# The first 512 tokens' q and k multiplied in f32 from the landed rows, six of nine blocks, held in PSUM until the scale is known

## The chip, the cores and the metric

The kernel runs on one core of one Trainium2 chip. The metric is device time in microseconds (us), the time of one launch of the whole program. Two kernels are compared by runs on the same chip, and one execution of each is recorded by the hardware profiler. Five engines work in parallel, each through its own instructions in order: TensorE (PE in the profile, with its weight loads as PEld) multiplies matrices into the eight banks of PSUM, VectorE (DVE), ScalarE (ACT) and GpSimd (POOL) work on elements, and SyncE (SP) issues most of the DMAs.

## The reference

Two independent operators over 2048 tokens of 576 features each, whose outputs stand side by side:

```
a: qkv = x @ wqkv                    x (2048, 576), wqkv (576, 1728)
   32 heads of 18; scores = q k^T / sqrt(18), only where 0 <= i - j < 256
   a = softmax(scores) v @ wo
b: K[d, l] = Re sum_n C[d,n] exp(dt_d A[d,n] l) dt_d B[d,n]     n = 0..127, l = 0..2047
   b = causal convolution over l of u (2048, 576) with K, plus u * Dskip
```

All inputs and outputs are f32.

## The kernel before

**Stages.** The program has a front (inputs, scales, splits of operands), a stage in which the projection qkv of operator a (`proj`), the tables and taps of K of operator b (`tables`) and the first step of the transform of u (`s1_u`) run together, and then the attention, into which the rest of the convolution and the output projection are woven.

**The projection.** A product of f32 operands is made from three products of f16 operands. An operand is multiplied by a power of two that depends on its largest absolute value, rounded to f16 (`wh`, `xh`), and the rest is kept in a second f16 tile (`wl`, `xl`). `mm14` (L173) makes one block: 128 columns of wqkv against 512 tokens, over 576 rows in five slices (the fifth has 64 rows, stored twice, so that its second half can carry a residual): five products wh xh, five wl xh and four wh xl, 14 in all, into one bank. A chunk of 512 tokens has nine blocks of q and k (m = 0 to 8) and four of v (tk = 0 to 3, two halves of 288 columns each, operands exchanged). A q/k block leaves its bank as f16 plus residual, one ScalarE and one VectorE instruction (L345, L346), and goes to DRAM by six DMAs of SP (`store_heads`). There are four chunks.

**The scales** need the largest value of all of wqkv and of all of x. `front` (L217) loads wqkv in four parts of 432 columns (the K tile, L229), the first 512 tokens of x transposed (`raw`, four tiles, L240) and the other 1536 tokens flat (`flat`, four pieces in two buffers, L237). VectorE reduces each as it lands (`amax`), GpSimd reduces over the partitions (`pow2_max`), VectorE makes the power of two (`pow2_of`). `split_w` makes wh on ScalarE and wl on VectorE, `split_x` the same of x. Between them stand the `level` steps, which split the exponents of operator b into three bf16 parts by way of small DMAs on the queues of ScalarE and GpSimd (into `al` and `ps`), and the first exponentials (`exps_ab`, `exps_q`): an outer product on PE (L376) into one of two xps banks, then an Exp on ScalarE (L393).

**What sets the order.** The front is under `manual_schedule`: its instructions keep the order in which they are written, on each engine and queue. Of the next stage only the order of the generators' steps is written (`merge`, first six steps of `proj` and four of `tables`, then 50, 308 and 16 of `proj`, `tables`, `s1_u`); the planner orders the instructions by its own costs and may start some while the front still runs. Each engine then takes its instructions in that fixed order. The attention is under `manual_schedule` again.

**PSUM.** Eight banks in the shared stage: pps 3 (projection and s1_u), xps 2 (outer products), trig 2 (sn and cs, which ScalarE writes for the tables), kps 1 (kp, the taps).

**The tables.** For each of 36 groups c: `factors` (two outer products, a fraction on ScalarE and VectorE, two Sin, then GpSimd, L424 to L435), `phases`, `qtable` (Sin into sn and cs, four VectorE products into Q), `products` (two GpSimd instructions, L446) and `taps` (64 small f32 products on PE into kp, L484). After every second group kp goes to the tile K (L490), which lies in the room that held wqkv.

The lines that matter beside the functions below are these, of `front`:

```python
for c in range(4):
    nc.sync.dma_start(wf[:, c], a["wqkv"][:, c])
...
    if c == 1:
        raw = [self.load_x(e, "prep", "raw%d" % e) for e in range(4)]
...
for e in range(4):
    self.split_x(raw[e], self.xs, e)
self.split_w(2, 0)
self.split_w(3, 0)
```

## Time and profile before

| what | value |
|---|---|
| median of 3 runs | 989.41 us (987.56 to 995.23) |
| the profiled execution | 989.74 us, span 988.0 us |
| busy in the span | PE 834.1, VectorE 666.0, GpSimd 567.5, ScalarE 565.7 us |
| mean granted clock of PE | 0.977 |
| scale of the weights known | 31.09 us |
| scale of x known | 49.98 us |
| first q/k block on PE | 53.06 us |
| last taps leave kp | 411.4 us |

The span runs from the first instruction to the last; the execution's own time has a little more around it. In a row of instructions stand the start in us, the time in us, engine, line, operation, output<-inputs, shapes and count, and in brackets the idle time before it and what ended it. Rows of groups (line first) have the busy us and the mean ns of one, then the idle time before. PE's products are pipelined and their ends are modelled, so products overlap in the rows and the distance of their starts says more than their length. The row of a transposing or splitting helper has the helper's line, not its caller's.

### The profile page before, as it was taken

Reading aid. Unit: us, or ns where it says so; the run is one execution under the profiler, and the core shown is the slowest. Engines: PE = TensorE matmul, PEld = TensorE weight load, DVE = VectorE, ACT = ScalarE, POOL = GpSimd, SP = SyncE. Lnnn points to the kernel's source line nnn. Section 1 sums busy time; section 2 is a strip of 40 time slices with the busy share of each in tenths; the row PEclk is TensorE's granted clock in tenths of the full one; section 3 lists DMA queues with packets and bytes.
Section 4 is the critical chain, followed back from the end, with each engine's and each line's share of the span. In section 5 each row is a group of like instructions: output and inputs, shape, how many; then the busy total and the mean of one; then the engine's idle time right before and its main releaser. Section 6 shows DMA issues by size and latency. Waiting matters only on the chain.

```text
span 988.0 us, 26891 instructions
## 1 busy us (share of the span) xinstructions
PE 834.1 (84%) x10364; PEld 443.4 (45%) x10364; DVE 666.0 (67%) x1784; ACT 565.7 (57%) x917; POOL 567.5 (57%) x674
## 2 busy tenths in 40 slices
PE   0287979898899899889988888888888899999987
PEld 0033645465457466644433333333333344444445
DVE  5689496556754774666586788788777766667534
ACT  1455756557767666325655655665556555665770
POOL 2118575465875785802257775866686756644460
PEclk9999989899999999999999999999999999999999
DMA  9825535344444343354584675756755664387663
GB/s 307 255 57 138 124 93 146 87 98 116 102 104 120 89 106 107 106 185 151 170 156 120 165 190 137 172 144 167 179 137 143 158 194 104 108 223 196 205 195 130
DMA packets 137177, 145.34 MB, mean 147 GB/s; under 512 B 36552, under 2 KB 105336, under 8 KB 136280
## 3 DMA queue, kind: packets, MB, share of 16 engines
q1 hardware_dynamic: 131000, 131.45, 49.6%
q0 software_dynamic: 4592, 10.32, 3.8%
q10 hardware_dynamic: 1456, 1.84, 0.6%
q8 instruction: 82, 1.34, 0.6%
q14 instruction: 47, 0.39, 0.1%
HBM read 81.29 MB, written 61.01 MB: 144 GB/s over the span
## 4 chain that ended last, share of the span: by engine, by line
PE 47%; DVE 20%; issue 11%; ACT 7%; DMA 7%; POOL 6%; SPq 2%; DVEq 0%; ACTq 0%; POOLq 0%
PE pp L180 9%; PE po L764 6%; PE r L700 5%; PE r L974 5%; PE kp L484 4%; PE pp L525 3%; PE r L566 3%; PE r L574 3%; PE ST L741 3%; DVE jk L707 3%; PE x L376 2%; PE r L525 2%; POOL P L752 2%; ACT P L743 2%; DMA c_ct<-in_c_ct_dram 2%
## 5 line engine op out<-in xcount | busy, mean ns | idle before, releaser
L707 DVE CUSTOM_DVE_ANT_0 jk<-r,bias 128x288 f32<-128x288 f32 (+7 forms) x512 | 199.8, 433 | 92.8 <-PE r L700 88.3
L752 POOL TENSOR_SCALAR_AFFINE_SELECT P<-P 128x512 f32<-128x512 f32 x240 | 166.3, 722 | 156.6 <-ACT P L743 154.2
L743 ACT ACTIVATE P<-ST,esc 128x1024 f32<-128x1024 f32 (+1 forms) x192 | 202.0, 1059 | 84.2 <-PE ST L741 83.9
L446 POOL TENSOR_TENSOR m<-A,tr 128x1024 f32<-128x1024 f32 x72 | 144.2, 2025 | 83.6 <-PE kp L484 77.7
L700 PE MATMUL r<-K,qb 128*64 128x288 f16 (+7 forms) x1024 | 130.0, 294 | 36.8 <-DVE qb L691 12.2
L700 PEld LDWEIGHTS <-qb 128*64 128x64 f16 x1024 | 57.6, 108 | 122.2 <-issue 68.5
L764 PE MATMUL po<-P,V 128*32 128x256 f32 (+2 forms) x1408 | 100.0, 396 | 13.3 <-ACT osb L772 5.1
L603 POOL TENSOR_TENSOR Y<-t,t 64x288 f32<-64x288 f32 x64 | 55.1, 861 | 66.0 <-DVE t L598 64.0
L484 PE MATMUL kp<-Q,m 128*32 128x64 f32 x4608 | 80.6, 222 | 10.2 <-ACT K L490 2.6
L484 PEld LDWEIGHTS kp<-Q,m 128*32 128x32 f32 x4608 | 69.4, 110 | 41.2 <-issue 24.0
L741 PE MATMUL ST<-Q,K 64*128 64x384 f16 (+2 forms) x704 | 73.0, 280 | 1.2 <-DMA Q<-mt 1.2
L180 PE MATMUL pp<-xh,wh 128*128 128x512 f16 x180 | 50.0, 397 | 9.5 <-ACT xh L211 8.9
L424 POOL TENSOR_TENSOR tr<-tr,mab 128x768 f32<-128x768 f32 x18 | 33.6, 1867 | 41.7 <-ACT tr L393 41.7
L764 PEld LDWEIGHTS po<-P,V 128*32 128x32 f32 x1408 | 35.8, 110 | 48.3 <-issue 28.9
L387 DVE TENSOR_TENSOR k<-x,k 128x512 f32<-128x512 f32 (+1 forms) x54 | 34.0, 641 | 33.3 <-ACT k L386 32.7
L180 PEld LDWEIGHTS <-wh 128*128 128x128 f16 x324 | 31.9, 100 | 53.5 <-issue 21.0
L604 POOL TENSOR_TENSOR Y<-t,t 64x288 f32<-64x288 f32 x64 | 52.0, 813 | 3.8
L180 PE MATMUL pp<-xh,wl 128*128 128x512 f16 x180 | 49.9, 404 | 0.0
L388 DVE TENSOR_SCALAR ab<-k 128x512 int32<-128x512 int32 (+1 forms) x54 | 47.5, 892 | 0.4
L346 DVE SCALAR_TENSOR_TENSOR qst<-pp,qst 128x512 f16<-128x512 f32 x36 | 24.6, 684 | 34.1 <-ACT qst L345 27.9
L525 PE MATMUL pp<-ut,w 128*128 128x288 f32 x128 | 40.6, 440 | 7.8 <-DVE qst L346 5.6
L566 PE MATMUL r<-tx,w 128*64 128x288 f32 x256 | 41.1, 430 | 5.7 <-DVE m L707 3.8
(174 smaller groups left out, 1664.1 us busy)
## 6 DMA issues: line engine op xcount, KB each, us to landing
qd<-qst SPq DMA_DIRECT2D x72, 128.0 KB
gx<-g SPq DMA_DIRECT2D x32, 288.0 KB
gk<-g SPq DMA_DIRECT2D x32, 288.0 KB
tx<-gx SPq DMA_DIRECT2D x32, 288.0 KB
tk<-gk SPq DMA_DIRECT2D x32, 288.0 KB
h<-ho SPq DMA_DIRECT2D x16, 576.0 KB
Q<-qd SPq DMA_DIRECT2D x32, 216.0 KB
raw<-in_x_dram SPq DMA_DIRECT2D x16, 320.0 KB
```

The lines of the kernel that those rows point to most:

```text
L180: self.nc.tensor.matmul(ps, u, v, start=(i == 0), stop=(i == len(ops) - 1))
L446: self.nc.gpsimd.tensor_tensor(m, A[:, ch, a0:a0 + 8].unsqueeze(3).to_broadcast(sh), tr[:, ch, part, 0:8].unsqueeze(2).to_broadcast(sh), o ...
L484: nc.tensor.matmul(kp[32 * st:32 * st + 32, c % 2 * JJ2 + j, :], m[:, ch, a0:a0 + 32], Q[:, ch, term % 2, :], start=(term == 0), stop=(ter ...
L525: nc.tensor.matmul(ps, self.w1[:, part, :], src[:, o:o + k], start=True, stop=True)
L566: nc.tensor.matmul(ps[64 * par:64 * par + 64], w2[:, par, 64 * part:64 * part + 64], t[:, par, 2 * hs:2 * hs + 2, :], start=True, stop=True)
L603: nc.gpsimd.tensor_tensor(Y[par][0:64], t1[sl, 0], t2[sl, 0], op=OP.subtract)
L700: nc.tensor.matmul(ps[64 * b:64 * b + 64, :n], self.qb[:, b, t, :], d["K"][:, b, k0:k0 + n], start=True, stop=True, skip_group_check=True)
L707: nc.vector.tensor_tensor_reduce(out=jk[:, :n], in0=ps[:, :n], in1=self.bias[:, 288 - n:], scale=1.0, scalar=-3e38, op0=OP.add, op1=OP.max ...
L741: nc.tensor.matmul(ps[:, u, o:o + n], d["K"][h, jp, k0:k0 + 128], d["Q"][h, jp, q0:q0 + n], start=True, stop=True, skip_group_check=True)
L743: nc.scalar.activation(pt[:, 2 * jp:2 * jp + 2, lo:hi], ps[:, :, lo:hi], AF.Exp, scale=self.esc)
L752: nc.gpsimd.affine_select(v, v, pattern=[[0, 4], [sg, 128]], compare_op=OP.is_ge, fill=0.0, base=-1 if far else 0, channel_multiplier=-sg)
L764: nc.tensor.matmul(self.po[32 * j:32 * j + 32, t0 * 128:t1 * 128], V[:, kb * 76 + 19 * j:kb * 76 + 19 * j + 32], pt[:, j, o:o + (t1 - t0) ...
```

## The change

The first six of the nine q/k blocks of the first 512 tokens no longer use the split operands. They are multiplied in f32 straight from the landed weights and the landed raw rows, five products each, before either scale is known (`exact`), and stay in six PSUM banks: three of pps, both of trig, and kp. When the scales are known, the eviction (`heads`) multiplies by `qsc`, the scales' product with 2^-24, in place of 2^-24. 15 of the 30 products are issued ahead of the reductions, the others in turn with the exponentials.

For that wqkv now lies as three parts of 384 columns (q and k) and one of 576 (v); raw is one tile and is loaded right behind the first weight part, ahead of the other three. In the front the raw rows are reduced between the weight parts, and parts 2 and 3 are split instead of 0 and 1; parts 0 and 1, which chunk 0 no longer needs, are split in the shared stage. The order of chunk 0 puts the v blocks between the evictions of the held blocks. The K tile is claimed at its first write instead of at the start of `proj`.

```diff
     def split_w(self, c, part):
-        cs = slice(c * 432, c * 432 + 432)
+        cs = slice(c * 384, c * 384 + (576 if c == 3 else 384))
...
+    NH = 6
+
+    def exact(self, raw):
+
+
+        ps = [self.p["pps"].tile([128, 512], F32, name="pp") for _ in range(3)]
+        ps += [self.p["trig"].tile([128, 512], F32, name=n) for n in ("sn", "cs")]
+        ps.append(self.p["kps"].tile([128, 512], F32, name="kp"))
+        self.held = ps
+        for m in range(self.NH):
+            ks = [0, 1, 2, 3, 4] if m % 2 == 0 else [4, 0, 1, 2, 3]
+            for i, k in enumerate(ks):
+                r = slice(0, 128) if k < 4 else slice(64 * (m % 2), 64 * (m % 2) + 64)
+                self.nc.tensor.matmul(ps[m], self.wf[m // 3][r, k, m % 3 * 128:m % 3 * 128 + 128], raw[r, :, k, :],
+                                      start=(i == 0), stop=(i == 4))
+                yield
...
-        wf = self.wf = self.p["K"].tile([128, 4, 5, 432], F32, name="K")
+        wt = self.p["K"].tile([128, 8640], F32, name="K")
+        wf = [wt[:, 1920 * c:1920 * c + (2880 if c == 3 else 1920)] for c in range(4)]
+        self.wf = [w.rearrange("p (k n) -> p k n", k=5) for w in wf]
+        raw = tp.tile([128, 4, 5, 128], F32, name="raw")
         for c in range(4):
-            nc.sync.dma_start(wf[:, c], a["wqkv"][:, c])
+            nc.sync.dma_start(wf[c], a["wqkv"][:, 1920 * c:1920 * c + (2880 if c == 3 else 1920)])
+            if c == 0:
+                for e in range(4):
+                    nc.sync.dma_start(raw[:, e], a["x"][:, e])
...
-            if c == 1:
-                raw = [self.load_x(e, "prep", "raw%d" % e) for e in range(4)]
...
         exps = chain(self.exps_ab(0), self.exps_ab(1), self.exps_q(0))
+        exact = self.exact(raw)
+        for _ in range(15):
+            next(exact)
         for c in range(4):
-            self.amax(amx[:, c:c + 1], wf[:, c])
+            self.amax(amx[:, c:c + 1], wf[c])
             if c < 3:
                 level(c)
+            if c < 2:
+                for e in (2 * c, 2 * c + 1):
+                    self.amax(amx[:, 4 + e:5 + e], raw[:, e])
         wm, wg = self.pow2_max(amx[:, 0:4], "w")
         pw, self.sw = self.pow2_of(wg, "w")
-        next(exps), next(exps)
-        self.split_w(0, 0)
-        next(exps), next(exps)
-        self.split_w(1, 0)
+        steps = chain.from_iterable(zip(exps, exact))
+        for _ in range(4):
+            next(steps), next(steps)
+        self.split_w(2, 0)
         self.amax(amx[:, 8:9], flat[0])
-        self.split_w(0, 1)
+        self.split_w(2, 1)
         for _ in range(4):
-            next(exps)
+            next(steps), next(steps)
+        self.split_w(3, 0)
         self.amax(amx[:, 9:10], flat[1])
-        for c in range(4):
-            self.amax(amx[:, 4 + c:5 + c], raw[c])
-        self.split_w(1, 1)
+        for _ in range(4):
+            next(steps), next(steps)
+        for _ in chain(steps, exact):
+            pass
+        self.split_w(3, 1)
         for c in range(2, 4):
             self.amax(amx[:, 8 + c:9 + c], flat[c])
-        for _ in exps:
-            pass
         xm, xg = self.pow2_max(amx[:, 4:12], "x")
         px, self.sx = self.pow2_of(xg, "x")
+        self.qsc = sp.tile([128, 1], F32, name="qsc")
+        nc.vector.scalar_tensor_tensor(self.qsc, self.sx, 2.0 ** -24, self.sw, op0=OP.mult, op1=OP.mult)
+        nc.vector.tensor_scalar(self.qsc, self.qsc, 3e38, None, op0=OP.min)
         self.xs = self.x_tiles()
         for e in range(4):
-            self.split_x(raw[e], self.xs, e)
-        self.split_w(2, 0)
-        self.split_w(3, 0)
+            self.split_x(raw[:, e], self.xs, e)
...
+        def heads(m, ps, scale):
+            st = self.p["pst"].tile([128, 2, 512], F16, name="qst")
+            nc.scalar.activation(st[:, 0], ps, AF.Copy, scale=scale)
+            nc.vector.scalar_tensor_tensor(st[:, 1], ps, scale, st[:, 0], op0=OP.mult, op1=OP.subtract)
+            for e in range(2):
+                self.store_heads(st[64 * e:64 * e + 64], 2 * m + e, cs)
+
+        def qk(m):
+            if c == 0 and m < self.NH:
+                heads(m, self.held[m], self.qsc)
+                return
+            ps = self.p["pps"].tile([128, 512], F32, name="pp")
+            self.mm14(ps, (wh, wl), (xh, xl), slice(m * 128, m * 128 + 128), slice(0, 512))
+            heads(m, ps, S)
...
+        order = [[(qk, m) for m in range(9)] + [(v, t) for t in range(4)]] * 4
+        order[0] = [(qk, 0), (qk, 1), (v, 0), (qk, 2), (v, 1), (qk, 3), (v, 2), (qk, 4), (v, 3), (qk, 5),
+                    (qk, 6), (qk, 7), (qk, 8)]
...
+            for n, (f, i) in enumerate(order[c]):
+                f(i)
+                if c == 0 and 2 <= n < 6:
+                    self.split_w((n - 2) // 2, n % 2)
+                if c < 3 and n < 8:
+                    if n % 2 == 0:
+                        t = self.load_x(4 * c + 4 + n // 2)
                     else:
-                        self.split_x(t, self.xs, m // 2)
-                yield
...
         if c % 2:
             q = c // 2
+            if q == 0:
+                self.K = self.p["K"].tile([128, 64, 144], F32, name="K")
```

The function `v` that the order names is the old loop body over tk, unchanged.

More of the change, by code (lines that the diff above doesn't have):

```diff
@@ L195, in split_w @@
     def split_w(self, c, part):
-        cs = slice(c * 432, c * 432 + 432)
+        cs = slice(c * 384, c * 384 + (576 if c == 3 else 384))
         wh, wl = self.w
         if part == 0:
-            self.nc.scalar.activation(wh[:, :, cs], self.wf[:, c], AF.Copy, scale=self.sw)
+            self.nc.scalar.activation(wh[:, :, cs], self.wf[c], AF.Copy, scale=self.sw)
         else:
-            self.nc.vector.scalar_tensor_tensor(wl[:, :, cs], self.wf[:, c], self.sw, wh[:, :, cs],
+            self.nc.vector.scalar_tensor_tensor(wl[:, :, cs], self.wf[c], self.sw, wh[:, :, cs],
                                                 op0=OP.mult, op1=OP.subtract)
+    NH = 6
[11 more added lines that the diff above has]
+                yield
     def x_tiles(self):
@@ L332, in proj, with v @@
         (wh, wl), vst = self.w, self.vst
-        self.K = self.p["K"].tile([128, 64, 144], F32, name="K")
         S = 2.0 ** -24
+        def heads(m, ps, scale):
[11 more added lines that the diff above has]
+            heads(m, ps, S)
+        def v(tk):
+            v = vst[tk % 2]
+            for hf in range(2):
+                ps = self.p["pps"].tile([128, 512], F32, name="pp")
+                w0 = 1152 + hf * 288
+                self.mm14(ps[:, :288], (wh, wl), (xh, xl), slice(w0, w0 + 288),
+                          slice(tk * 128, tk * 128 + 128), flip=True)
+                nc.scalar.activation(v[:, 16 * hf:16 * hf + 16, 0:18],
+                                     ps[:, :288].rearrange("p (h d) -> p h d", d=18), AF.Copy, scale=S)
+            nc.sync.dma_start(self.vd[:, :, 4 * c + tk].rearrange("g p e -> p g e"),
+                              v.rearrange("p (g h) d -> p g (h d)", g=8))
+        order = [[(qk, m) for m in range(9)] + [(v, t) for t in range(4)]] * 4
+        order[0] = [(qk, 0), (qk, 1), (v, 0), (qk, 2), (v, 1), (qk, 3), (v, 2), (qk, 4), (v, 3), (qk, 5),
+                    (qk, 6), (qk, 7), (qk, 8)]
         for c in range(4):
@@ L340, in proj @@
             yield
-            for m in range(9):
-                ps = self.p["pps"].tile([128, 512], F32, name="pp")
-                self.mm14(ps, (wh, wl), (xh, xl), slice(m * 128, m * 128 + 128), slice(0, 512))
-                st = self.p["pst"].tile([128, 2, 512], F16, name="qst")
-                nc.scalar.activation(st[:, 0], ps, AF.Copy, scale=S)
-                nc.vector.scalar_tensor_tensor(st[:, 1], ps, S, st[:, 0], op0=OP.mult, op1=OP.subtract)
-                for e in range(2):
-                    self.store_heads(st[64 * e:64 * e + 64], 2 * m + e, cs)
-                if c == 0 and m < 2:
-                    self.split_w(2 + m, 1)
-                if c < 3 and m < 8:
-                    if m % 2 == 0:
-                        t = self.load_x(4 * c + 4 + m // 2)
-                    else:
-                        self.split_x(t, self.xs, m // 2)
-                yield
-            for tk in range(4):
-                v = vst[tk % 2]
-                for hf in range(2):
-                    ps = self.p["pps"].tile([128, 512], F32, name="pp")
-                    w0 = 1152 + hf * 288
-                    self.mm14(ps[:, :288], (wh, wl), (xh, xl), slice(w0, w0 + 288),
-                              slice(tk * 128, tk * 128 + 128), flip=True)
-                    nc.scalar.activation(v[:, 16 * hf:16 * hf + 16, 0:18],
-                                         ps[:, :288].rearrange("p (h d) -> p h d", d=18), AF.Copy, scale=S)
-                nc.sync.dma_start(self.vd[:, :, 4 * c + tk].rearrange("g p e -> p g e"),
-                                  v.rearrange("p (g h) d -> p g (h d)", g=8))
+            for n, (f, i) in enumerate(order[c]):
[5 more added lines that the diff above has]
+                        t = self.load_x(4 * c + 4 + n // 2)
+                    else:
+                        self.split_x(t, self.xs, n // 2)
                 yield
@@ L1088 @@
         "xf": np.ascontiguousarray(inputs["A_x"][0, 512:].reshape(128, -1)),
-        "wqkv": columns(inputs["A_wqkv"][:, np.r_[np.arange(1152).reshape(64, 18).T.ravel(), 1152:1728]], 432),
+        "wqkv": np.concatenate([columns(w, n).reshape(128, -1) for w, n in (
+            (inputs["A_wqkv"][:, np.arange(1152).reshape(64, 18).T.ravel()], 384), (inputs["A_wqkv"][:, 1152:], 576))], 1),
         "wo": np.zeros((128, 5, D), np.float32),
```

## The prediction

> **What bounds the kernel now.** I read the page first, then the busy time of each engine by stage, then the chain of waits up to 130 us, and last the instructions of the first 110 us in order of time. On the page TensorE (PE) leads by a wide margin. The stage table (each engine's busy us, granted clock, DMA share, GB/s) says where.
>
> ```profile
> PE 834.1 (84%) x10364; PEld 443.4 (45%) x10364; DVE 666.0 (67%) x1784; ACT 565.7 (57%) x917; POOL 567.5 (57%) x674
> ```
>
> ```profile
> core 0: us, PE busy (x) PEld busy (x) DVE busy (x) ACT busy (x) POOL busy (x), PEclk, DMA share, GB/s
> 0.00:53.00 53.00, 7.11 (x15) 1.77 (x16) 33.04 (x37) 18.50 (x27) 11.34 (x27) 1.00 0.84 266
> 53.00:74.50 21.50, 20.91 (x86) 8.96 (x86) 18.02 (x27) 10.84 (x14) 2.85 (x3) 1.00 0.28 59
> 74.50:106.00 31.50, 23.33 (x357) 12.77 (x356) 28.76 (x39) 19.40 (x35) 27.47 (x24) 0.95 0.45 117
> 106.00:411.00 305.00, 279.77 (x5396) 176.52 (x5394) 190.30 (x283) 195.42 (x358) 199.88 (x156) 0.97 0.42 107
> ```
>
> Four regimes. Until 53 us PE idles for 45.9 of 53 us. From 53 to 74.5 it is full. From 74.5 to 106 VectorE (DVE) is the tightest (28.76 of 31.5) and PE has 8.2 us to spare. From 106 to 411, the rest of the projection and table stage, PE is the bound at 92%, no other engine over 66%. The change touches all four. The attention behind 411 us it doesn't touch.
>
> The first regime is not paced by PE. The chain of waits (start, us, what) has DMA and then one long piece that the chain calls issue; VectorE's own rows show what fills that piece.
>
> ```profile
> 6.09 17.73 DMA c_ct<-in_c_ct_dram
> 30.33 18.49 issue
> ```
>
> ```profile
> 8.05 2.40 DVE L170 TENSOR_REDUCE amx<-K 128x1 f32<-128x2160 f32 x1
> 22.34 2.40 DVE L170 TENSOR_REDUCE amx<-K 128x1 f32<-128x2160 f32 x1
> 24.77 0.16 DVE L154 TENSOR_REDUCE wm<-amx 128x1 f32<-128x4 f32 x1
> 31.01 2.54 DVE L170 TENSOR_REDUCE amx<-flat 128x1 f32<-128x2304 f32 x1
> 35.85 2.47 DVE L201 SCALAR_TENSOR_TENSOR wl<-K,wr,wh 128x2160 f16<-128x2160 f32 x1 [2.30 <-ACT wh L199]
> 40.70 2.99 DVE L170 TENSOR_REDUCE amx<-raw 128x1 f32<-128x640 f32 x4
> 45.98 2.61 DVE L170 TENSOR_REDUCE amx<-flat 128x1 f32<-128x1152 f32 x2
> 49.83 0.15 DVE L166 TENSOR_SCALAR xr<-xr 128x1 f32<-128x1 f32 x1
> 55.43 4.85 DVE L201 SCALAR_TENSOR_TENSOR wl<-K,wr,wh 128x2160 f16<-128x2160 f32 x2
> 66.08 0.74 DVE L320 TENSOR_TENSOR wi<-in_C_re,in_C_im 128x576 f32<-128x576 f32 x1
> ```
>
> The weights' scale comes first, the scale of x is known at 49.98, and only then can x be split and PE start (53.06 in the row below). The changed kernel lets PE work before either scale.
>
> **The change part by part.** Prices of the blocks, from the chain's pieces (a piece is the time until PE's next work, so x8 of L525 is four f32 products, two records each) and from PE's rows:
>
> ```profile
> 348.19 1.94 PE pp L525 x8
> 369.14 3.02 PE pp L180 x14
> 125.08 3.43 PE pp L180 x28
> ```
>
> ```profile
> 32.45 0.80 PE L376 MATMUL x<-c_ca,al 96*128 96x384 bf16 x2 [32.45 <-DMA al<-part]
> 53.06 1.86 PE L180 MATMUL pp<-xh,wh 128*128 128x512 f16 x4 [8.92 <-ACT xh L211]
> 74.23 0.33 PE L376 MATMUL x<-c_ca,ps 96*128 96x384 bf16 x1
> 87.39 0.32 PE L484 MATMUL kp<-Q,m 128*32 128x64 f32 x8
> 143.87 0.48 PE L376 MATMUL x<-c_ca,al 96*128 96x384 bf16 x1 [5.73 <-ACT sn L393]
> ```
>
> and the stage table once more, for eight us after that last pause:
>
> ```profile
> 142.00:150.00 8.00, 6.13 (x22) 2.48 (x22) 6.24 (x12) 5.12 (x9) 1.26 (x3) 0.50 0.48 143
> ```
>
> Removed: six f16 blocks of 14 products, 3.02 us each, 18.1 us. They are the first six, which ran from 53.06 to 74.23, 21.2 us with their slow start (four products in 1.86 us, twice 3.02/14).
>
> Added: 30 f32 products over 512 columns. One over 288 columns takes 1.94/4 = 0.485 us, so one takes 0.485 x 512/288 = 0.86 us and all 30 take 25.9 us. The other end is a PE at half clock, as the four products from 53.06 ran and as the last row above grants it: 1.72 us. I take 0.86 for the first 15, since 15 in a row keep PE busy. The fifth slice of each block has only 64 rows; I take nothing off for it.
>
> ```profile
> raw<-in_x_dram SPq DMA_DIRECT2D x16, 320.0 KB
> ```
>
> The first 15 need the first weight part, reduced from 8.05 on, and four such loads of x, 1.31 MB, 4.9 us at 266 GB/s: some 13 to 26 us. They hide in idle PE time before 32.45, where PE waits for a DMA, and cost nothing; without that cover they would cost their 12.9 us.
>
> The other 15 alternate on PE with the outer products that start at 32.45, and these feed ScalarE's exponentials, which stand ahead of the weight split on ScalarE, which stands ahead of VectorE's second half of the split and of the reductions of x. Here the added work is on the path. First the weights' scale:
>
> ```profile
> 28.03 1.96 POOL L276 DMA_DIRECT2D ps<-part  x4 [4.32 <-ACT part L272]
> 30.02 0.31 POOL L155 PARTITION_ALL_REDUCE wg<-wm  x1
> ```
>
> The four reductions of raw x (2.99 us) move ahead of it, so wm goes from 24.77 to 27.8, still under 29.99, when POOL is done with its queue. The 1.31 MB pushed ahead of weight parts 1 to 3 on SP's queue cost at most 4.9 us: the last reduction goes from 22.34 to 27.2 at the latest, takes 3.2 us for 2880 columns and ends at 30.4. So the scale comes between 0 and 0.9 us later; I take 0.4.
>
> ```profile
> L199 ACT ACTIVATE wh<-K,wr 128x2160 f16<-128x2160 f32 x4 | 8.3, 2092 | 0.0
> L393 ACT ACTIVATE mab<-x 128x384 f32<-128x384 f32 x4 | 1.7, 492 | 5.2 <-PE x L376 5.2
> L393 ACT ACTIVATE mg<-x 128x512 f32<-128x512 f32 x8 | 4.4, 601 | 0.6 <-PE x L376 0.6
> ```
>
> PE has paused by then, and after the 5.73 us pause above its granted clock stays at 0.50 from 142 to 150. So I take the first products at half clock: from 32.45 four outer products at 0.4 and three f32 products at 1.72 bring 39.2; the fourth exponential ends near 39.7. Split of part 2 on ScalarE (1920 of 2160 columns, 1.86): 41.6; VectorE's half (2.47 x 1920/2160 = 2.2): 43.8; second reduction of flat (2.54): 46.3. ScalarE meanwhile does four exponentials (2.4) and part 3 (2.79) until 46.8; VectorE's half of it (3.3): 50.1; last reductions 2.61: 52.7; then, as from 48.59 to 49.98, 1.4: the scale of x at 54.1, with the 0.4 at 54.5, 4.5 us later than now. Bounds: 1 us later if PE is warm throughout, 10 us later if all 15 run at half clock (13 us more on PE, part of it beside the splits).
>
> The rule that speaks against this is in the Trainium skill, page "TensorE: Matmul & The Clock Gate", section "Part 1: The HAM clock gate": after about 3.4 us without work PE falls to half clock, and some 3.4 us of work bring it back. The trace agrees on the halving and shows a longer stretch than the page. By the page two products would be slow, not three, and the sum below would come out 1 us better.
>
> Next, a wait is added: the three pps banks, both trig banks and kp are held until ScalarE and VectorE have read the block out. On PE the v blocks queue behind the first free pps bank, and everything else on PE behind them. ScalarE has four x splits and one exponential first.
>
> ```profile
> 50.02 2.98 ACT L211 ACTIVATE xh<-raw,xr 128x640 f16<-128x640 f32 x4 [6.67 <-DVE xr L166]
> 56.88 0.67 ACT L309 ACTIVATE dt<-dt 128x576 f32<-128x576 f32 x1
> 59.32 0.60 ACT L345 ACTIVATE qst<-pp 128x512 f16<-128x512 f32 x1 [1.05 <-PE pp L180]
> 74.87 0.60 ACT L345 ACTIVATE qst<-pp 128x512 f16<-128x512 f32 x1 [2.91 <-DMA qd<-qst]
> 83.32 0.58 ACT L393 ACTIVATE sn<-k 128x512 f32<-128x512 f32 x1
> ```
>
> So the first bank is read near 58.2 (54.5 + 2.98 + 0.67 for the exponential) and free near 61, behind VectorE's share of the x splits (until 55.4 now), and PE restarts there, not at 53. Six such evictions take (74.87 - 59.32)/5 = 3.1 us each, with their stores; at that pace the banks of sn and cs are free near 72 and kp near 75. They are wanted at 83.32 and 87.39, so this wait is covered by 11 us and would cost what exceeds them.
>
> VectorE from 53 to 106: weight parts 0 and 1 (4.4 us) are split there in place of 2 and 3 (4.85 at 55.43); all else is the same work. So its chain to wi (66.08) and on to the tables keeps its length and moves by the 4.5 us. ScalarE has 1.86 us twice in place of 4.2: nothing. The K tile is now claimed only at its first write; that costs nothing, since parts 0 and 1 are read long before.
>
> PE from 61 to 110.5: of chunk 0 it now has three q/k blocks and four v blocks, 9.1 + 13.7 = 22.8 us, where it had nine blocks, 27.2 us, before 106. Its other work there is 20.91 + 23.33 - 27.2 = 17 us. With 4 us for a restart at half clock that is 44 in 49.5 us: it fits, so by 110.5 the v blocks (13.7 us; one pair is the 3.43 at 125.08), which now run from 105 to 129, are already done. Behind it PE's relief counts at 92%: 12.6 us.
>
> Sum against the profiled execution (989.74 us around a span of 988.0; the median of three is 989.41): -12.6 + 4.5 = -8.1, so 981.6, or 981 on the median. Own range 975 to 988: the scale's bounds and a relief of 60 to 130%.
>
> **The rivals.** *All of it arrives (chance 0.20).* If chunk 1's x is split earlier, PE has work for all of its gaps, and the whole 21.2 us stretch of the six blocks goes, less 4.5: 973. For it: PE is at 92% behind 106. Against it: VectorE is busy for 46.8 of the 53 us before.
>
> *A wait in its place (0.20).* If the freed PE time in 61 to 110 goes idle, since v waits for banks that free one in 3.1 us and outer products queue behind v, about half of the v blocks are left at 110: -6.3 + 4.5, so 988. For it: six of eight banks are held. Against it: the 5 us that fit above.
>
> *Slower (0.15).* The table groups, not PE, set the pace behind 106: each is a chain PE, ScalarE, VectorE, POOL, PE. Then freed PE time is worth nothing, and the end moves by as much as the first group does, from 4.5 us up, plus what the held kp bank adds if its eviction, ordered behind the last v block, comes after 87.39. It decides from a scale of x later than 66 us on, where the 11 us of cover are gone. Price 4.5 to 12, likeliest 6: 996. For it: the first groups have no slack on VectorE. Against it: behind 106 VectorE is busy for 190 of 305 us.
>
> **How the numbers follow.** The forecast has 0.45: the time is 981. What can be told from no change here is about 1%, 9.9 us, so the lines are 979.5 and 999.3. Faster by more: all of the first rival and some 0.16 of the forecast's 0.45, for 981 lies near the line: 0.36. Slower by more: a third of the last rival and something for the order of work that the planner picks afresh: 0.07. Within: 0.57. The range takes the forecast, nearly all of the first two rivals and half of the last: 970 to 995.
>
> **What would show it.** Right: PE busy with K and raw x before 30 us; xr at 51 to 56; first v product at 58 to 63; first sn no later than 86; chunk 0's last v before 100; PE at over 90% from 110 on, and the table stage ending near 403. Wrong: xr behind 60 (the scale chain); first kp behind 92 (the held banks); PE under 85% between 60 and 400 (the tables' own pace).

## The result, and the profile after

The changed kernel takes 977.16 us (median of 18, 970.72 to 987.38) beside 989.15 for the kernel before on the same chip (median of 18): a ratio of 0.9881, 95% interval 0.9854 to 0.9908. That is 11.8 us less, with 9.1 to 14.4 us inside the interval. Ratios leave out slow executions, those more than 1.5% above the fastest of their kernel, here only the profiled one. The forecast was 981 in a range of 970 to 995.

The profiled execution took 987.38 us around a span of 985.7. A second one of the same kernel, called *again* below, took 982.28 us; both lie above their medians, at a granted clock of 0.965 and 0.967, so I read places in the program from them, and times from the medians.

First the page of the changed kernel (busy time of each engine), then its stage table: stretch, length, busy time and instructions of PE, PEld, DVE, ACT and POOL, granted clock, DMA share, GB/s. The last two stretches are cut at the fourth write of K from kp and at the end of the last.

```profile
PE 844.3 (86%) x10340; PEld 448.5 (46%) x10340; DVE 662.9 (67%) x1786; ACT 566.0 (57%) x917; POOL 568.6 (58%) x674
```

```profile
0.00:53.00 53.00, 32.07 (x69) 12.57 (x70) 33.41 (x29) 19.98 (x24) 9.75 (x22) 0.94 0.78 243
53.00:74.50 21.50, 11.67 (x65) 7.40 (x64) 18.09 (x37) 11.66 (x20) 4.06 (x6) 0.76 0.46 129
74.50:106.00 31.50, 25.40 (x471) 17.15 (x469) 28.25 (x40) 20.16 (x40) 27.64 (x26) 0.95 0.54 144
106.00:152.00 46.00, 40.92 (x783) 23.50 (x784) 30.84 (x50) 35.09 (x64) 32.04 (x24) 1.00 0.51 130
152.00:397.20 245.20, 226.66 (x4442) 142.64 (x4440) 153.95 (x234) 157.65 (x289) 167.93 (x134) 0.98 0.41 103
```

The same cut of the kernel before, whose fourth write of K comes at 165:

```profile
106.00:165.00 59.00, 52.72 (x952) 33.21 (x951) 35.34 (x50) 38.01 (x70) 30.63 (x23) 0.91 0.47 121
165.00:411.00 246.00, 227.05 (x4445) 143.31 (x4443) 154.96 (x234) 157.41 (x289) 169.25 (x134) 0.98 0.41 104
```

Everything that the table stage gains is gained before the fourth write of K: from there to the last write both kernels take about the same time (246.0 and 245.2 us) with the same work. From 53 us to the last write of K, PE's work fell from 324.01 to 304.65 us (-19.4), and its idle time rose from 34.0 of 358 us to 39.6 of 344.2 (+5.6): the end of the table stage moved by -13.8. The new idle time is in 53 to 74.5 (+9.2), where PE now works 11.67 of 21.5 us, at a granted clock of 0.76; behind that PE idles 3.7 us less than before.

The steps, from the changed kernel's instructions in order of time (start, us, engine, line, operation, output<-inputs; in brackets the idle time before and what ended it):

```profile
14.97 14.74 PE L217 MATMUL pp<-raw,K 128*128 128x512 f32 x30 [14.97 <-DMA raw<-in_x_dram]
...
55.91 0.15 DVE L166 TENSOR_SCALAR xr<-xr 128x1 f32<-128x1 f32 x1
...
64.99 1.36 PE L180 MATMUL pp<-wh,xh 128*128 128x288 f16 x5 [9.83 <-DVE qst L367]
...
67.52 0.75 DVE L349 TENSOR_TENSOR wi<-in_C_re,in_C_im 128x576 f32<-128x576 f32 x1
...
90.64 0.40 ACT L386 ACTIVATE vst<-pp 128x288 f32<-128x288 f32 x1
...
95.45 3.70 PE L525 MATMUL kp<-Q,m 128*32 128x64 f32 x249
101.49 1.02 ACT L533 ACTIVATE K<-kp 128x512 f32<-128x512 f32 x1
...
396.22 1.04 ACT L533 ACTIVATE K<-kp 128x512 f32<-128x512 f32 x1 [3.84 <-PE kp L525]
```

The last half v block of the first 512 tokens leaves its bank at 90.64. In the kernel before, this row and the last write of K were

```profile
128.80 0.39 ACT L364 ACTIVATE vst<-pp 128x288 f32<-128x288 f32 x1
410.37 1.03 ACT L490 ACTIVATE K<-kp 128x512 f32<-128x512 f32 x1 [5.36 <-PE kp L484]
```

The first products of taps come 8 us later than before (95.45 against 87.39), the first write of K 3.9 us later (101.49 against 97.60), and the last 14.2 us earlier.

### The profile page after: what moved, and what is told of

Its sections match the earlier page's. It is cut to its first block, busy times and chain, and to the rows that moved or that the text cites. A ratio compares the mean times of both kernels' runs of the same rounds, so it can differ in the third digit from the quotient of the medians.

```text
span 985.7 us, 26852 instructions
## 1 busy us (share of the span) xinstructions
PE 844.3 (86%) x10340; PEld 448.5 (46%) x10340; DVE 662.9 (67%) x1786; ACT 566.0 (57%) x917; POOL 568.6 (58%) x674
## 3 DMA queue, kind: packets, MB, share of 16 engines
q10 hardware_dynamic: 1456, 1.84, 0.7%
## 4 chain that ended last, share of the span: by engine, by line
PE 45%; DVE 21%; issue 11%; ACT 8%; DMA 7%; POOL 5%; SPq 2%; DVEq 0%; ACTq 0%; POOLq 0%
PE pp L180 8%; PE po L807 6%; PE r L743 6%; PE r L1017 5%; PE kp L525 4%; PE r L609 3%; PE pp L568 3%; PE ST L784 3%; PE r L617 3%; DVE jk L750 3%; PE r L568 2%; PE x L417 2%; ACT P L786 2%; DVE qb L734 2%; DVE osb L866 2%
## 5 line engine op out<-in xcount | busy, mean ns | idle before, releaser
L743 PE MATMUL r<-K,qb 128*64 128x288 f16 (+7 forms) x1024 | 130.9, 298 | 41.6 <-DVE qb L734 12.2
L807 PE MATMUL po<-P,V 128*32 128x256 f32 (+2 forms) x1408 | 100.4, 397 | 12.7 <-ACT osb L815 4.4
L646 POOL TENSOR_TENSOR Y<-t,t 64x288 f32<-64x288 f32 x64 | 54.5, 852 | 67.6 <-DVE t L641 65.7
L617 PE MATMUL r<-Y,i 128*128 128x288 f32 x128 | 42.8, 448 | 3.9 <-DVE t L642 1.2
L145 ACT ACTIVATE g<-pp 128x288 f32<-128x288 f32 x69 | 26.7, 412 | 32.5 <-PE pp L568 31.2
L609 PE MATMUL r<-tk,w 128*64 128x288 f32 x256 | 40.8, 424 | 4.8 <-DVE m L750 4.7
L434 ACT ACTIVATE mg<-x 128x512 f32<-128x512 f32 x72 | 39.9, 600 | 7.2 <-PE x L417 6.8
L367 DVE SCALAR_TENSOR_TENSOR qst<-pp,qst 128x512 f16<-128x512 f32 x30 | 20.6, 686 | 34.8 <-ACT qst L366 31.0
```

The lines of the kernel that those rows point to most:

```text
L609: nc.tensor.matmul(ps[64 * par:64 * par + 64], w2[:, par, 64 * part:64 * part + 64], t[:, par, 2 * hs:2 * hs + 2, :], start=True, stop=True)
L617: nc.tensor.matmul(pair[par], i1[:, par, :], Y[par], start=True, stop=True)
L743: nc.tensor.matmul(ps[64 * b:64 * b + 64, :n], self.qb[:, b, t, :], d["K"][:, b, k0:k0 + n], start=True, stop=True, skip_group_check=True)
L807: nc.tensor.matmul(self.po[32 * j:32 * j + 32, t0 * 128:t1 * 128], V[:, kb * 76 + 19 * j:kb * 76 + 19 * j + 32], pt[:, j, o:o + (t1 - t0) ...
```

## The experiments

All theories agree that PE has less to do. They differ in what holds the beginning: the f32 products between the exponentials (later scale of x), the held banks, or something that came along with them. The table has, per kernel, four places from its profiled execution, then the median and its ratio to the kernel before on the same chip. "x scale" is the start of the last instruction of xr, "wi" the start of the last step of VectorE's chain of parameters (see below), "4th K" and "last K" the fourth and the last write of K.

| kernel | x scale | wi | 4th K | last K | median us | ratio, 95% |
|---|---|---|---|---|---|---|
| before | 49.83 | 66.08 | 165.1 | 410.4 | | |
| changed | 55.91 | 67.52 | 152.0 | 396.2 | 977.16 | 0.9881 (0.9854 to 0.9908) |
| again | 54.34 | 65.95 | 151.4 | 395.8 | 976.37 | 0.9865 (0.9815 to 0.9915) |
| noexact | 47.41 | 64.15 | 159.0 | 404.9 | 985.89 | 0.9975 (0.9940 to 1.0010) |
| fifth | 52.94 | 64.54 | 148.3 | 394.1 | 976.98 | 0.9877 (0.9826 to 0.9929) |
| slope | 49.28 | 65.53 | 163.7 | 402.2 | 989.77 | 0.9974 (0.9938 to 1.0010) |
| later | 51.43 | 63.04 | 148.6 | 392.7 | 979.50 | 0.9862 (0.9823 to 0.9901) |
| first20 | 48.22 | 59.82 | 144.2 | 388.2 | 973.81 | 0.9815 (0.9784 to 0.9846) |
| held3 | 51.84 | 63.45 | 157.8 | 403.6 | 984.50 | 0.9925 (0.9895 to 0.9955) |
| evict_first | 54.14 | 65.74 | 149.9 | 394.9 | 976.70 | 0.9840 (0.9812 to 0.9869) |
| combo | 49.17 | 60.78 | 145.9 | 391.8 | 973.23 | 0.9832 (0.9776 to 0.9888) |
| warm | 47.72 | 64.46 | 158.2 | 403.5 | 988.76 | 0.9947 (0.9904 to 0.9990) |
| relief0 | 50.63 | 66.87 | 158.1 | 401.7 | 985.12 | 0.9942 (0.9911 to 0.9973) |
| delay | 63.22 | 74.82 | 159.7 | 405.6 | 986.48 | 0.9968 (0.9932 to 1.0003) |

*again* to *slope* ran on one chip, *later* to *evict_first* on another, *combo* to *delay* on a third (medians of the kernel before 990.07, 993.41 and 992.24), so kernels are compared by their ratios.

### again: the changed kernel once more

No edit.

> The changed kernel once more, for a second profile. Theory A (PE bounds the table stage, so the 18.1 us of f16 products taken out of it arrive at its end, less what the later scale of x costs): 11 to 13 us under the kernel before; in the profile the last write of K ends near 397 us as in the first profile of the change (411.4 before), and the rest of the program takes the 577 us that it takes before, not the 588 of that first profile. Rival B (the gain comes from the other edits: loads, the place of the reductions, the late claim of the K tile, the order of chunk 0) and rival C (the tables' own chain sets the pace and PE's freed time is worth little) expect the same time here; they part in the next three.

Ratio 0.9865, as on the first chip, so the gain is the kernel's and not one chip's. The last write of K came where it was expected; the rest of the program took 583.7 us, between the 576.6 of before and the 588.4 of the first profile, and not the 577 expected (see *slope and relief0*).

### noexact: the new loads and the late claim of K, without held blocks

```diff
-    NH = 6
+    NH = 0
-        for _ in range(15):
-            next(exact)
...
+        next(exps), next(exps)
+        self.split_w(0, 0)
+        next(exps), next(exps)
+        self.split_w(1, 0)
         self.amax(amx[:, 8:9], flat[0])
-        self.split_w(2, 1)
+        self.split_w(0, 1)
...
+        self.split_w(2, 0)
+        self.split_w(3, 0)
```

> The changed kernel without the held f32 blocks: all nine blocks of chunk 0 in f16 as before, splits and order of chunk 0 as before; raw behind the first weight part, the parts of 384 and 576 columns, the raw reductions between the weight parts and the late claim of K stay. Theory A: no gain, -2 to +2 us against the kernel before; scale of x at 49 to 51. Rival B: 8 to 12 us faster than before. Rival C: no gain either.

The scale of x comes 2.4 us earlier than before and the time is not distinguishable from it (0.9940 to 1.0010). What came along with the held blocks is worth at most some 6 us, most likely 2.5, so most of the gain is in the held blocks. It need not be nothing: *warm* below has no held blocks either and is 5.3 us faster than before (1.0 to 9.6), and in both profiles the fourth write of K (159.0 and 158.2) stands 6 to 7 us before that of the kernel before, the last one 5.5 and 6.9. Against *noexact* the held blocks bring some 9 to 11 us of time, and 8.7 to 9.1 at the last write of K.

### fifth: one product of five in the held blocks

Four of the five products are left out of each of the first six q/k blocks of the first 512 tokens.

```diff
             for i, k in enumerate(ks):
+                if i:
+                    yield
+                    continue
...
-                                      start=(i == 0), stop=(i == 4))
+                                      start=True, stop=True)
```

> The changed kernel with one f32 product of five in each held block; four fifths of the rows of those six blocks are left out, so q and k of the first 512 tokens are not the reference's. It takes 20.6 us of f32 work out of the front. Theory A with the scale's delay priced in full (6.1 us later in the first profile): scale of x at 50 to 51 instead of 56.06, and 4 to 6 us faster than the changed kernel, 16 to 18 under before. Rival: the delay is hidden because PE bounds the end and has work left anyway: 0 to 2 us faster than the changed kernel.

With a fifth of the f32 work left, the scale of x is 1.4 us earlier than in *again* and 3.0 earlier than in the first profile of the changed kernel, the last write of K 1.7 and 2.1, and the time is the same within its interval of some 5 us either way. So the 26 us of f32 products, as such, cost some 2 us in place, and no more than that interval in time. But *noexact* has the scale another 5.5 us earlier. Something else than f32 products can hold it there; the rows of ScalarE and VectorE in *again* show what.

```profile
33.59 1.89 ACT L199 ACTIVATE wh<-K,wr 128x1920 f16<-128x1920 f32 x1
...
38.05 1.89 ACT L199 ACTIVATE wh<-K,wr 128x1920 f16<-128x1920 f32 x1
39.84 0.48 ACT L434 ACTIVATE mab<-x 128x384 f32<-128x384 f32 x1
40.21 1.89 ACT L199 ACTIVATE wh<-K,wr 128x1920 f16<-128x1920 f32 x1
...
44.63 2.69 ACT L199 ACTIVATE wh<-K,wr 128x2880 f16<-128x2880 f32 x1
```

```profile
35.51 2.22 DVE L201 SCALAR_TENSOR_TENSOR wl<-K,wr,wh 128x1920 f16<-128x1920 f32 x1 [3.44 <-ACT wh L199]
39.97 4.38 DVE L201 SCALAR_TENSOR_TENSOR wl<-K,wr,wh 128x1920 f16<-128x1920 f32 x2 [2.24 <-ACT wh L199]
44.27 2.55 DVE L170 TENSOR_REDUCE amx<-flat 128x1 f32<-128x2304 f32 x1
47.35 3.22 DVE L201 SCALAR_TENSOR_TENSOR wl<-K,wr,wh 128x2880 f16<-128x2880 f32 x1 [0.53 <-ACT wh L199]
50.48 2.61 DVE L170 TENSOR_REDUCE amx<-flat 128x1 f32<-128x1152 f32 x2
...
54.34 0.15 DVE L166 TENSOR_SCALAR xr<-xr 128x1 f32<-128x1 f32 x1
...
65.95 0.75 DVE L349 TENSOR_TENSOR wi<-in_C_re,in_C_im 128x576 f32<-128x576 f32 x1
```

All four weight parts are split ahead of the scale of x: three of 1920 columns and one of 2880. The source writes only parts 2 and 3 there and gives parts 0 and 1 to the shared stage; the planner, which may start work of that stage while the front runs, put them into the gaps that ScalarE has between the exponentials. With the f32 products in place these gaps are there anyway; without them (*fifth*) the extra splits fill the same time. That is how I read the rows; no run took the extra splits alone away. And what is split before the scale needn't be split behind it: in every kernel with held blocks wi starts 11.6 us behind xr (54.34 to 65.95 here), while before it was 16.25 (49.83 to 66.08, with 4.85 us of splits between). So the later scale, +4.5 us in *again*, doesn't make VectorE's chain later at all: -0.1.

### slope and relief0: less PE work alone

The kernel before, with 5 of 14 products in six q/k blocks: nine products each are left out, 11.6 us at 3.02/14 each, in the third chunk (*slope*) or in the first (*relief0*).

```diff
+        ops = ops[:n]
...
-                self.mm14(ps, (wh, wl), (xh, xl), slice(m * 128, m * 128 + 128), slice(0, 512))
+                self.mm14(ps, (wh, wl), (xh, xl), slice(m * 128, m * 128 + 128), slice(0, 512),
+                          n=5 if c == 2 and m < 6 else 14)
```

In *relief0* the last line has `c == 0`.

> The kernel before, with 5 products of 14 in the first six q/k blocks of chunk 2: the products with the residual tiles are left out there, so those q and k have f16 precision. It takes 54 products of 0.2155 us, 11.6 us, off PE in the middle of the table stage and changes nothing else. Theory A: 9 to 12 us faster than before, the last write of K that much earlier. Rival C: 0 to 3 us.

> The kernel before with 5 products of 14 in the first six q/k blocks of chunk 0 instead of chunk 2; the residual products are left out, so those q and k have f16 precision. 11.6 us off PE between 53 and 75 us, nothing else. If relief in chunk 0 is what the change brings (15 to 17 us from the first to the fourth write of K): fourth write of K 8 to 11 us before 165.1, last one too, time 6 to 10 us under before. If it only moves PE's idle time, as VectorE sets the pace to 106 us: 0 to 3 us.

At the last write of K 8.2 (slope) and 8.6 us (relief0) of the 11.6 have arrived, some 70 to 75%, though 1.4 of slope's 8.2 stand ahead of its edit, at the fourth write (163.7 against 165.1). Over all runs the time is shorter by 5.8 us (2.7 to 8.8) in *relief0* and by 2.6 (between 6.1 less and 1.0 more) in *slope*. At the 92% of the prediction it would be 10.7; neither interval reaches that. The fourth write of K in *relief0* stands 7.0 us before that of the kernel before, where 8 to 11 were expected, and hardly before those of *warm* and *noexact*, which take nothing off PE.

```profile
401.74 1.03 ACT L492 ACTIVATE K<-kp 128x512 f32<-128x512 f32 x1 [4.81 <-PE kp L486]
464.40 0.59 ACT L774 ACTIVATE osb<-po 128x512 f32<-128x512 f32 x1
```

```profile
402.18 1.04 ACT L492 ACTIVATE K<-kp 128x512 f32<-128x512 f32 x1 [4.47 <-PE kp L486]
468.60 0.59 ACT L774 ACTIVATE osb<-po 128x512 f32<-128x512 f32 x1
```

The first fence is *relief0*, the second *slope*: from the last write of K to the attention's first write of osb (the first output rows to leave PSUM) one takes 62.7 us and the other 66.4. In the profiles of all kernels this stretch takes 60.7 to 71.7 us, 61.1 in the kernel before, 71.7 and 68.7 in the two profiles of the changed kernel. It goes with the granted clock in it, 0.94 in the six profiles of up to 62.8 us and 0.85 to 0.92 in the eight of 66.4 and more; both groups have kernels with and without held blocks, and which of the two, length or clock, brings the other isn't shown. What is gained ahead of it can be lost there in one execution; why so little of *slope* arrives over its runs stays open.

### later and first20: where the f32 products stand

*later* puts the second 15 products behind all exponentials. *first20* does the same with 10, and has 20 ahead.

```diff
-        for _ in range(15):
+        for _ in range(20):
             next(exact)
...
-        steps = chain.from_iterable(zip(exps, exact))
         for _ in range(4):
-            next(steps), next(steps)
+            next(exps)
```

*later* is this without the first two lines; the other calls of `next(steps)` and the last `chain` are changed likewise.

> The changed kernel with the second 15 f32 products on PE behind all twelve exponentials' outer products instead of in turn with them; nothing else moves. My step that these products delay the scale of x (54.3 to 55.9 in two profiles of the change, 52.9 with one product of five) expects the scale at 52.5 to 53.5, the first taps 2 us earlier than the change's 95 to 96, and 1 to 3 us less time than the change. Rival (the first table groups are held by the banks, not by the scale): scale as said, first taps unmoved, time within 1.5 us of the change.

> As the run with the second 15 behind the exponentials, but 20 products ahead of them and 10 behind: PE's pause between the 15th product (near 30 us) and the first outer product (34) is filled, and the last f32 product ends near 51 instead of 57. If PE's work before 60 us matters at all, 1 to 3 us less than that run; by the rival that it is idle time anyway, the same within 1.5 us.

The scale of x is 2.9 us earlier in *later* and 6.1 in *first20* than in *again*. That *first20* is the earlier of the two I read as the planner's choice again, not as its f32 work. Its rows:

```profile
29.42 3.68 ACT L199 ACTIVATE wh<-K,wr 128x1920 f16<-128x1920 f32 x2 [3.73 <-DVE wr L166]
33.01 1.75 ACT L433 ACTIVATE mab<-x 128x384 f32<-128x384 f32 x4
34.65 1.89 ACT L199 ACTIVATE wh<-K,wr 128x1920 f16<-128x1920 f32 x1
...
38.51 2.69 ACT L199 ACTIVATE wh<-K,wr 128x2880 f16<-128x2880 f32 x1
```

and the one of *later* that matters:

```profile
48.10 2.21 DVE L201 SCALAR_TENSOR_TENSOR wl<-K,wr,wh 128x1920 f16<-128x1920 f32 x1
```

In *first20* parts 0 and 1 are split right behind the weights' scale, while the exponentials still wait for al; in *later* one of them comes between the last reduction of x and the scale, and costs its 2.2 us in full. *first20* is the fastest ratio of all, 0.9815 (0.9784 to 0.9846): clear of the changed kernel's interval on the first chip, while it overlaps the wider one of *again*. *later* can't be told from the changed kernel.

### held3: three blocks instead of six

```diff
-    NH = 6
+    NH = 3
-        ps += [self.p["trig"].tile([128, 512], F32, name=n) for n in ("sn", "cs")]
-        ps.append(self.p["kps"].tile([128, 512], F32, name="kp"))
...
-        order[0] = [(qk, 0), (qk, 1), (v, 0), (qk, 2), (v, 1), (qk, 3), (v, 2), (qk, 4), (v, 3), (qk, 5),
+        order[0] = [(qk, 0), (qk, 1), (v, 0), (qk, 2), (v, 1), (v, 2), (v, 3), (qk, 3), (qk, 4), (qk, 5),
```

The other products stand behind all exponentials, as in *later*.

> Only the first three blocks in f32, in the pps banks; trig and kp are not held, blocks 3 to 5 of chunk 0 run in f16 behind the v blocks. Half the relief, 9.1 us of f16 products, and none of the wait for the trig and kp banks. If relief on PE is what counts: first taps 84 to 90, fourth write of K 154 to 158 (151.5 with six, 159.0 with none), 5 to 8 us under before, so 4 to 7 us over the change. Rival (the held trig and kp banks cost as much as blocks 3 to 5 bring): as fast as the change within 2 us.

Only pps banks are held, half the f16 work goes: 7.5 us (4.5 to 10.4) of gain against 13.7 (9.8 to 17.6) in *later* on the same chip. Holding the table banks too is worth it. In its profile, the slowest of its ten executions, the fourth and last writes of K stand only 1.2 and 1.3 us before those of *noexact*: the gain is not even over the blocks.

### evict_first and combo: the held banks read out before the v blocks

```diff
-        order[0] = [(qk, 0), (qk, 1), (v, 0), (qk, 2), (v, 1), (qk, 3), (v, 2), (qk, 4), (v, 3), (qk, 5),
+        order[0] = [(qk, 0), (qk, 1), (qk, 2), (qk, 3), (qk, 4), (qk, 5), (v, 0), (v, 1), (v, 2), (v, 3),
```

*combo* is *first20* with this edit.

> The changed kernel with all six evictions ahead of the v blocks in the order of chunk 0, so that trig and kp come free earlier. If the held banks delay the tables (first taps at 95 to 96 in the change, 82.2 without the held blocks): first taps at 84 to 90, and 2 to 6 us less time than the change. Rival (the tables wait for VectorE, not for the banks): first taps unmoved, time within 1.5 us.

> 20 f32 products ahead of the exponentials and 10 behind, and all six evictions ahead of the v blocks: the two edits joined. If they act on different things (scale of x from 54 to 48; banks of the tables' first group): first taps at 76 to 80, last write of K at 385 to 388, time 18 to 22 us under before (20 products alone: 0.9815). If both only bring the first group forward, and the group has another bound by then: as with 20 products alone, within 2 us.

In the changed kernel the held banks are read out on ScalarE at these times, with the wait that the cs bank made:

```profile
59.56 1.24 ACT L366 ACTIVATE qst<-pp,qsc 128x512 f16<-128x512 f32 x2
...
69.14 0.69 ACT L366 ACTIVATE qst<-pp,qsc 128x512 f16<-128x512 f32 x1
...
73.86 0.68 ACT L366 ACTIVATE qst<-sn,qsc 128x512 f16<-128x512 f32 x1
...
78.96 0.68 ACT L366 ACTIVATE qst<-cs,qsc 128x512 f16<-128x512 f32 x1
...
83.89 0.69 ACT L434 ACTIVATE cs<-ab,halfpi 128x512 f32<-128x512 f32 x1 [1.87 <-DVE qst L367]
...
90.07 0.67 ACT L366 ACTIVATE qst<-kp,qsc 128x512 f16<-128x512 f32 x1
```

With the evictions first, kp is read at 78.39 and the taps start 12 us earlier (96.08 in *again*):

```profile
83.86 3.41 PE L525 MATMUL kp<-Q,m 128*32 128x64 f32 x181
90.63 1.03 ACT L533 ACTIVATE K<-kp 128x512 f32<-128x512 f32 x1
...
149.88 1.02 ACT L533 ACTIVATE K<-kp 128x512 f32<-128x512 f32 x1
```

But the fourth write of K comes 1.5 us earlier than in *again* (2.1 earlier than in the first profile) and the last 0.9 (1.4). The ratio, 0.9840 (0.9812 to 0.9869), can't be told from *again*'s and overlaps that of the first chip, and *combo* is no better than *first20*. The wait for kp is real, 12 us long at the first taps, and worth some 2 us by the fourth write of K; the times leave room for more (0.9840 against 0.9881 is 4 us).

### warm: PE kept busy before the first exponentials

*noexact* with 20 f32 products, which nothing reads, ahead of the exponentials.

```diff
+        for _ in self.exact(raw):
+            pass
```

> The kernel without the held blocks (all nine blocks of chunk 0 in f16, new loads), with the same 20 f32 products ahead of the exponentials, whose results nobody reads. No relief on PE, only a PE that has worked by 32 us. If the clock explains why 20 products ahead beat 15 (scale of x 48.2 against 51.4): the outer products at 0.16 to 0.22 us apart instead of 0.4, scale of x at 45 to 46.5 (47.41 without), time 1 to 4 us under the kernel without held blocks (0.9975), ratio 0.993 to 0.997. If the gain is all relief: scale of x at 47 to 48, ratio as without.

The scale of x is 47.72 against 47.41. Here nothing is gained by a warm PE: the first two outer products take 0.49 us in place of 0.82, but PE then stands for 1.84 and 1.69 us between pairs, and from the seventh on a pair takes 1.07 as in *noexact*. The ratio can't be told from *noexact*'s. With the order of the splits read off the rows, the clock isn't needed to explain *first20* either.

### delay: the scale of x made later

The changed kernel with six further reductions of the last piece of x (1.3 us each) ahead of its scale.

```diff
-            self.amax(amx[:, 8 + c:9 + c], flat[c])
+            for _ in range(1 if c == 2 else 7):
+                self.amax(amx[:, 8 + c:9 + c], flat[c])
```

> The changed kernel with six more reductions of the last piece of flat (1.3 us each, 7.8 us) ahead of the scale of x: scale at 62 to 63.5, nothing else. It prices the scale's delay, which my sum took at its full size. In full: first taps, fourth and last write of K and the time 6 to 8 us later than the change (0.9865 to 0.988 of before becomes 0.994 to 0.996). If there is slack: 0 to 3 us.

From *again* to *delay* xr and wi move by 8.9 us, the last write of K by 9.8, and the ratio goes from 0.9865 to 0.9968, some 10 us (4 to 16 by the intervals). A delay that reaches VectorE's chain is paid in full. So is a gain: *first20* has wi 6.1 us earlier and the last K 7.6.

## Why the prediction was right, and where it was not

**The relief** was priced at 12.6 us (13.7 us of v blocks at 92%). The eight kernels that hold six blocks allow a check: if the time is the relief plus the shift of wi against before, then time gained plus that shift should be the same number for all. Gains are (1 - ratio) times the median of before on that chip:

| kernel | gain us | shift of wi | sum |
|---|---|---|---|
| changed | 11.8 | +1.4 | 13.2 |
| again | 13.4 | -0.1 | 13.3 |
| fifth | 12.2 | -1.5 | 10.7 |
| later | 13.7 | -3.0 | 10.7 |
| first20 | 18.4 | -6.3 | 12.1 |
| evict_first | 15.9 | -0.3 | 15.6 |
| combo | 16.7 | -5.3 | 11.4 |
| delay | 3.2 | +8.7 | 11.9 |

Mean 12.4, each within some 3 us, which is about what the intervals allow. The rule was found with these runs in hand, but the 12.6 was not. Yet it isn't a measurement of the v blocks or of the 92%. By the same rule the two kernels that take nothing off PE give 0.6 (*noexact*) and 3.6 (*warm*), which the sum had put at nothing; and *relief0* gives 6.6 and *slope* 2.0, where 92% of their 11.6 us would be 10.7. At the rate of *relief0*, half of what is taken off, the 18.1 us bring 9.0, and with *noexact*'s 2.5 that makes 11.5, as near to the 11.8 as the sum is. The runs show that the held blocks bring most of the gain; that the relief came out at its price is, as far as they tell, in part luck, a rate too high and other edits put at nothing.

**The failed term is the +4.5.** The step read: VectorE "from 53 to 106: weight parts 0 and 1 (4.4 us) are split there in place of 2 and 3 ... all else is the same work. So its chain to wi (66.08) and on to the tables keeps its length and moves by the 4.5 us." The scale did come 4.5 us later in *again* (6.1 in the first profile, where al landed 1.6 later), but the chain behind it was 4.6 us shorter, since parts 0 and 1 had been split ahead of the scale. The term is +1.4 in the first profile and -0.1 in *again*. With it the sum is -11.2 to -12.7, against -11.8 measured, the relief taken at its price. The forecast's own text says that the planner picks its order afresh; what it missed is that this applies to steps whose place the source seems to give.

**The scale of x, step by step.** Weights' scale "between 0 and 0.9 us later": it came 0.8 earlier (30.3 against 31.09): VectorE's last reduction ended at 28.9, inside the bound, and GpSimd came to its own at 29.20 instead of 30.02. From there, in *again*: part 2 on ScalarE until 42.1 (predicted 41.6), the second reduction of flat until 46.8 (46.3), VectorE's half of part 3 until 50.6 (50.1), last reductions until 53.1 (52.7), scale 54.5 (54.5). The chain holds to half a microsecond, although two further splits ran in it: they fell into gaps that the slow products had opened. The f32 products at half clock are there as well, three in *again*:

```profile
33.10 2.07 PE L217 MATMUL sn<-raw,K 64*128 64x512 f32 x2
...
35.40 1.91 PE L217 MATMUL sn<-raw,K 128*128 128x512 f32 x2
...
37.42 1.91 PE L217 MATMUL sn<-raw,K 128*128 128x512 f32 x2
...
39.39 1.02 PE L217 MATMUL sn<-raw,K 128*128 128x512 f32 x2
40.26 0.38 PE L417 MATMUL x<-c_cm,al 96*128 96x512 bf16 x1
```

From the fourth on, 0.87 us lie between a product and what follows it, 1.7 to 2.0 before. By the Trainium skill, page "TensorE: Matmul & The Clock Gate", section "Part 1: The HAM clock gate", PE comes back after about 3.4 us of sustained work. The trace agrees on the halving; in *again* the slow stretch of f32 products lasted 6.3 us (33.10 to 39.39) without a pause in the rows, the length that the sum used. In the first profile it began later, at 34.67, and ended near 39 us too: two slow products and one of 0.99 us.

**The price of f32** was right but for a slow start: 15 products took 14.74 us, where the prediction had 12.9, and stood from 14.97 to 29.7, where it had 13 to 26; they were done before the outer products needed PE.

**The held banks** were to be covered by 11 us, and would "cost what exceeds them". Of the two, the cover failed: the evictions stand between v blocks, which PE can't start before the first bank is free (64.9, not near 61, since VectorE has the x splits and four products of the parameters first) and does slowly at first (granted clock 0.76 from 53 to 74.5); so they are not 3.1 us apart, and kp is read at 90.07 instead of near 75. The sign that I had put down as speaking against the forecast, a first kp behind 92, was there: 95.45. *evict_first* shows that it costs some 2 us by the fourth write of K, not the 8 by which it exceeds 87.39. I read the rest as not lost because PE does the v blocks meanwhile, which have to be done anyway.

**The rivals.** "All of it arrives" (973) is as far from 977.2 as the forecast, and its 21.2 us of relief are not what the table shows. "A wait in its place" (988): PE did stand for 9.83 us before the first v block, but the v blocks are done by 91. The rest of chunk 0 isn't done by 110.5, as the forecast had it: its three f16 q/k blocks are read at 105.1, 110.7 and 120.3, and PE works 25.4 of 31.5 us from 74.5 to 106. "Slower" (996): the first taps did come later, but the fourth write of K is 13 us earlier, so the first group doesn't set the pace of the rest. *delay* shows how near it was: 9 us more on the scale take nearly all of the gain.

**The other signs.** First sn at 78.4 (by 86), chunk 0's last v at 90.6 (by 100), PE at 91.9% from 106 to the end of the table stage (over 90): as said. PE works 89% from 60 to 400, not under 85. First v at 64.99 and 63.42: outside 58 to 63. End of the table stage 397.3: six earlier than the 403. The shift that didn't happen is 3.1 of it in that profile; *noexact*, whose last write of K is 5.5 us before that of the kernel before, shows where the rest can come from.

## What to carry to other kernels

When a step is moved across a boundary between a hand-ordered stage and a planned one, find in the queue of each engine where it can end up, and price both places: here two splits cost 4.85 us behind the scale in the kernel before and, as I read the rows, nothing in the gaps of the changed kernel, while one of them cost 2.2 ahead of the scale in *later*. A later start of one value is not a later chain; price the chain to its last link. A wait on a resource that is released late can cost little, here some 2 of 12 us, when the engine that waits has other work that is due anyway. And a sum that comes out right doesn't prove its terms: price each with an edit that changes it alone.

## What the runs showed of the hardware

Two half-height f32 products run beside each other. The fifth slice of a block has 64 rows, and neighbouring blocks take theirs from different halves of the 128 rows and write different banks. In *first20*, where they meet:

```profile
27.38 0.69 PE L217 MATMUL pp<-raw,K 64*128 64x512 f32 x1
27.38 0.69 PE L217 MATMUL sn<-raw,K 64*128 64x512 f32 x1
27.91 0.59 PE L217 MATMUL pp<-raw,K 64*128 64x512 f32 x1
27.91 0.59 PE L217 MATMUL sn<-raw,K 64*128 64x512 f32 x1
```

Each f32 product has two records; both products start their first at 27.38 and their second at 27.91, so two of them take about 1.06 us instead of 2 x 0.86. One that stands alone takes as long, more than the 0.86 of a product of full height; in *again*:

```profile
48.16 1.12 PE L217 MATMUL kp<-raw,K 64*128 64x512 f32 x2
49.21 0.39 PE L417 MATMUL x<-c_cm,al 96*128 96x512 bf16 x1
```

The prediction had taken nothing off for this; over three pairs of six blocks that would be 2 us at most. In the changed kernel outer products stand between the products of two of the pairs, so one pair can meet at most. The Trainium skill's page "TensorEngine Tiling (Array Packing)", section "Overview", says that the array can be divided into independent parts when few rows are used, with up to twice the speed; the trace agrees, for f32 with 1.6 against two products at 0.86 and twice against two that stand alone.

The other is the spread. Over the 18 runs of the changed kernel the time goes with the mean granted clock: 970.72 us at 0.981, 987.38 at 0.965, some 10 us for each 0.01; which follows from which isn't shown. One profile of a kernel is therefore good for places in the program and not for a gain of 10 us.
